# Tiles 4 to 15 transposed by one DMA each, with copies of x behind them, in a Fourier-mixing and MLP kernel

## The chip, the cores and the metric

The kernel runs on one core of a Trainium2 chip. The metric is the device time of one execution in microseconds (us). The median of three runs before the change is 1255.71 us. Engines: TensorE (PE: matmuls and transposes by matmul; PEld is its loading of weights), VectorE (DVE), ScalarE (ACT), GpSimd (POOL) and SyncE (SP). SP only issues DMAs here: loads, copies in DRAM and transposing DMAs. POOL issues the DMAs that accumulate into DRAM.

## The reference

With x of 2048 rows and 576 columns, xn its layer norm, Cr, Ci the real and imaginary DFT matrices of the sequence and Dr, Di those of the hidden dimension:

```
xn  = (x - mean) / sqrt(var + 1e-5)
a   = xn @ Dr.T ;  b = xn @ Di.T
y   = Cr @ a - Ci @ b
out = x + y + relu(xn @ w1) @ w2        # w1: 576 x 4608, w2: 4608 x 576
```

All in f32. Each factor of a product is held as two f16 tensors, `hi` and `lo` (the rounded value and the remainder), after a scale by a power of two, so each product is three f16 products.

## The kernel before, in words

The 2048 rows are 16 tiles of 128, and 4 groups of 4 tiles. The MLP's 4608 columns are 9 blocks of 512. For each block b and group g there is a first product (`mlp1`, line 324, or `pair_products`, line 479, from block 2 on) and a second one (`mlp2`, line 556): seven products (q = 0 to 6) after Strassen and Winograd, 12 matmuls each, with sums of h and of w2 made by VectorE. After the MLP come the DFTs (lines 1091 and 1210).

A framework builds the program: it tracks which tile is written and read, sets the semaphores, and orders each engine's instructions by a list schedule on its own cost estimates, in which the order of the text is the priority. `tc.issue_after(ins)`, and `behind(key)` on top of it, put the instructions of a block behind `ins` on the queue of the same engine. Queues run in order.

The change lies in what comes before and inside block 0, the first 100 us:

- Tile t of x is loaded (line 96); `stats` makes mean and variance on VectorE (205, 208), a square root on ScalarE (215), then the reciprocal and a Newton step on VectorE (216 to 227).
- `normalize` writes xn in f32 on VectorE (247) and its f16 `hi` on ScalarE (249) into a staging buffer `dbuf`. `remainder` makes `lo` (253, 256), on POOL for tiles 1 to 11 and on VectorE for tile 0 and tiles 12 to 15.
- The transposed tile has ten blocks of 128 by 128: four and a half of `hi`, the same of `lo`, and the last 128 columns of `hi` once more. `transposes` (tiles 0 to 7) does them by ten matmuls (272, 277) into PSUM and two ScalarE copies (279, 282). `transposes_dma` (tiles 8 to 15) issues two transposing DMAs from SP: nine blocks (265), and one block that needs `hi` alone (266).
- Group 0 and half of group 1 take the first product tile by tile (`tile_by`), the other half 512 wide (`mlp1`). `mlp1_out` makes relu, `hi`, `lo` and the sums (365 to 377).
- `prepare_w2` makes w2's scale and splits: sums of magnitudes on ScalarE (646), a maximum over partitions by matmul (`power_pe`, 152 to 175), small VectorE steps (657 to 671), then for both halves i the splits (182 on ScalarE, 183 on VectorE) and sums (678 to 681). They are the steps `w[0]` to `w[10]` and beyond in the text.
- `mlp2` of block 0 and group 0 runs q = 0 to 2, then the first two `mlp1` of group 2 (`early`), then q = 3 to 6. Its results go to `acc` (567, 570), and POOL adds them into DRAM buffers `spill` (573).
- `spill` is first filled with x: 16 copies from DRAM to DRAM, 288 KB each (line 760), issued on SP behind all loads of x.
- In the loop after that, the step n == 2 takes group 2 and prepares tiles 12 to 15. Block 1's w1 (107) and w2 (100) are loaded through SP there, w2 into buffers which the splits of block 1's w1 free. `first_c` (948) loads blocks of the sequence matrices for their scale.

Of the kernel before, what the change touches and what calls it, by code (L numbers as in the profile page):

```python
# [14 lines left out]
ALU = mybir.AluOpType  # L15
# [34 lines left out]
def kernel(  # L50
# [101 lines left out]
    def power_pe(s, p, m):  # L152

        n = m.shape[-1]
        ps = ps2.tile([P, 2, 512], F32, tag="ps2", name="pm")

        for c in range(n):
            nc.tensor.matmul(
                ps[:1, 0, c * P : (c + 1) * P], m[:, c : c + 1], ident.bitcast(BF16),
                start=True, stop=True,  # L160
            )
        top = small.tile([1, n], BF16, tag=f"top{n}", name="top")
        nc.vector.tensor_reduce(
            top, ps[:1, 0, : n * P].rearrange("p (n f) -> p n f", f=P), AX.X, ALU.max
        )
        nc.tensor.matmul(ps[:, 1, :n], ones, top, start=True, stop=True)
        half = small.tile([P, n], F32, tag=f"half{n}", name="half")
        nc.vector.tensor_scalar(half, ps[:, 1, :n], 2.0**-107, 2.0**6, ALU.max, ALU.mult)
        nc.vector.tensor_scalar(
            s.bitcast(I32), half.bitcast(I32), EXPONENT, EXPONENT,  # L170
            ALU.bitwise_and, ALU.bitwise_xor,
        )
        nc.vector.tensor_scalar(
            p.bitcast(I32), half.bitcast(I32), EXPONENT, None, ALU.bitwise_and
        )
# [4 lines left out]
    def split(hi, lo, src, s):  # L180

        nc.scalar.activation(hi, src, AF.Copy, scale=s)  # L182
        nc.vector.scalar_tensor_tensor(lo, src, s, hi, ALU.mult, ALU.subtract)  # L183


    xT = [xpool[g].tile([P, NKX + 1, G], F16, name=f"xT{g}") for g in range(NG)]
# [7 lines left out]

        return tc.issue_after(order[key]) if key in order else nullcontext()

    def stats(ts, after=None):

        n = len(ts)
        mv = small.tile([P, n, 2], F32, tag=f"mv{n}", name=f"mv{ts[0]}")  # L200
        sts = [small.tile([P, 2, 6], F32, tag="st", name=f"st{t}", bufs=4) for t in ts]
        for t, st in zip(ts, sts):
            for j in range(2):
                with behind(after):
                    nc.vector.bn_stats(st[:, j, :], acc[t][:, j * EH : (j + 1) * EH])
                yield
        for i, st in enumerate(sts):
            nc.vector.bn_aggr(mv[:, i], st.rearrange("p a b -> p (a b)"))
# [6 lines left out]
        order["root", ts[0]] = nc.scalar.activation(u, v, AF.Sqrt, bias=eps).ins  # L215
        nc.vector.reciprocal(r0, u)
        yield

        stt(u, v, EPS, r0, ALU.add, ALU.mult)
        yield  # L220
        nc.vector.tensor_tensor(u, u, r0, ALU.mult)
        yield
        nc.vector.tensor_scalar(u, u, -0.5 * SX, 1.5 * SX, ALU.mult, ALU.add)
        yield
        nc.vector.tensor_tensor(r, u, r0, ALU.mult)
        yield
        order["sh", ts[0]] = stt(sh, m, -1.0, r, ALU.mult, ALU.mult).ins
        for i, t in enumerate(ts):
            means[t], factors[t], shifts[t] = mv[:, i, 0:1], r[:, i : i + 1], sh[:, i : i + 1]
# [12 lines left out]
    def normalize(t, eng=nc.vector, after=None):  # L242
        stage = dbufs[t % 4]
        xn = xns[t] = stage[:, :D]

        xs = xss[t] = stage[:, D : 2 * D].bitcast(F16)
        eng.tensor_scalar(xn, acc[t], means[t], factors[t], ALU.subtract, ALU.mult)
        with behind(after):
            nc.scalar.activation(xs[:, :D], acc[t], AF.Identity, bias=shifts[t], scale=factors[t])

    def remainder(t, eng):
# [2 lines left out]
            xs[:, D : D + REM], xn[:, KM * P :], xs[:, KM * P : D], ALU.subtract  # L254
        )
        eng.tensor_tensor(
            xs[:, D + REM :], xn[:, : KM * P], xs[:, : KM * P], ALU.subtract
        )

    def transposes_dma(t):  # L260

        xs = xss[t]
        g, c = divmod(t, TG)
        dst = xT[g][:, :, c * P : (c + 1) * P]
        nc.sync.dma_start_transpose(dst[:, :NKX], xs)
        nc.sync.dma_start_transpose(dst[:, NKX], xs[:, D - P : D])

    def transposes(t):
        xs = xss[t]
        pt = ps2.tile([P, 2, 1024], F16, tag="ps2", name=f"pt{t}")  # L270
        for k in range(NKX):
            nc.tensor.transpose(
                pt[:, k // 8, (k % 8) * P : (k % 8 + 1) * P], xs[:, k * P : (k + 1) * P], ident
            )
        g, c = divmod(t, TG)

        nc.tensor.transpose(pt[:, 1, P : 2 * P], xs[:, D - P : D], ident)
        dst = xT[g][:, :, c * P : (c + 1) * P]
        nc.scalar.activation(
            dst[:, :8, :], pt[:, 0, :].rearrange("p (k t) -> p k t", t=P), AF.Copy  # L280
        )
        order["xT", t] = nc.scalar.activation(
            dst[:, 8:, :], pt[:, 1, : 2 * P].rearrange("p (k t) -> p k t", t=P), AF.Copy
        ).ins

# [71 lines left out]
    def mlp1_out(b, g, i, pa, pb, after=None):  # L357
# [8 lines left out]
        for q, src in ((slice(A11, A11 + 1), a11), (slice(A12, A22 + 1), pb)):  # L366
            hi, lo = (h[:, n, q].rearrange("p a b -> p (a b)") for n in range(2))
            with behind(after):
                nc.scalar.activation(hi, src, AF.Relu)
            stt(lo, src, 0.0, hi, ALU.max, ALU.subtract)  # L370
        stt(s3, a11, 0.0, r21, ALU.max, ALU.subtract)
        stt(s1, a22, 0.0, r21, ALU.max, ALU.add)
        stt(s2, a22, 0.0, s3, ALU.max, ALU.subtract)
        stt(s4, a12, 0.0, s2, ALU.max, ALU.subtract)
# [167 lines left out]
    def mlp2(b, g, n):  # L542
# [25 lines left out]
        else:  # L568
            o = sums[row, col]
            add = nc.vector.scalar_tensor_tensor(o, ps, us[b], o, ALU.mult, ALU.add)  # L570
            order["acc"] = order["vfree"] = add.ins
        if n not in (0, 2, 3):
            nc.gpsimd.dma_start(spill[g, row, col], o, accum_op=ALU.add)  # L573

# [2 lines left out]
    def max_w1(b, f):  # L577
# [6 lines left out]
        with behind("vfree" if b >= BB else ("sh", 1) if f > 1 else None):  # L584
# [65 lines left out]
    def power_w2(b):  # L650
# [2 lines left out]
            yield from power(*(t["w2", b] for t in (sc, pw, mx)))  # L653
        else:
            m = small.tile([P, NQ], BF16, tag="mb2", name=f"mb2_{b}")
            with behind(("sh", 8)):
                nc.vector.tensor_copy(m, mx["w2", b])
            power_pe(sc["w2", b], pw["w2", b], m)
        p1 = pw["w1", b]
# [26 lines left out]
    def split_w2(b, i, c):  # L686
# [5 lines left out]
        with behind(None if b else ("xT", 7)):  # L692
            split(w[:, 0, q], w[:, 1, q], src, sc["w2", b][:, i : i + 1])

    def long(f):

# [58 lines left out]
    load_w2(0, 1)  # L755
    for t in range(2 * TG, NT):
        load_x(t)
    for g, row, col in spill:
        src = x[(g * TG + row * 2) * P : (g * TG + row * 2 + 2) * P, col * EH : (col + 1) * EH]
        nc.sync.dma_start(spill[g, row, col], src.rearrange("(c p) e -> p c e", p=P))  # L760
    warm = const.tile([P, 1], F32, name="warm")
    nc.scalar.activation(warm, eps, AF.Sqrt)

# [6 lines left out]
            mlp1_group(0, g, i, slice(c * P, (c + 1) * P), ps[i], wk)  # L770

    no = lambda: None
    N, E, T, TD = normalize, remainder, transposes, transposes_dma

    def fill(n, src=idle):

# [31 lines left out]
    E(2, GP)  # L808
    tile_by(0, (2,), ps)
    tile_by(1, (2,), ps)  # L810
    T(2)
    split_w1(0, 3)
    N(3)
    E(3, GP)
    tile_by(0, (3,), ps)
    tile_by(1, (3,), ps)
    T(3)
    weave(stats([4, 5, 6, 7]))
    N(4)
    E(4, GP)  # L820
# [11 lines left out]
    T(5)  # L832
    tile_by(4, (0, 1), qs)
    mlp1_out(0, 0, 0, *ps[:2])
    T(6)
    tile_by(5, (0, 1), qs)
    T(7)
    weave(stats([8, 9, 10, 11], ("sh", 4)))
    N(8, after=("xT", 5))
    E(8, GP)  # L840
    mlp1_out(0, 0, 1, *ps[2:], after=("xT", 6))
    for t in (9, 10, 11):
        N(t, after=("xT", 7))
        E(t, GP)
    tile_by(6, (0, 1), qs)
    w[3]()
    tile_by(7, (0, 1), qs)
    w[4]()
    w[5]()
    mlp1_out(0, 1, 0, *qs)  # L850
    for f in w[6:]:
        f()
    TD(8)
    q2 = [mlp1(0, 1, 2)]
    TD(9)
    q2.append(mlp1(0, 1, 3))
    mlp1_out(0, 1, 1, *q2)
    TD(10)
    TD(11)
    for q in range(3):  # L860
        mlp2(0, 0, q)
    with tc.issue_after(order["pe"]):
        early = [mlp1(0, 2, 0), mlp1(0, 2, 1)]
    for q in range(3, 7):
        mlp2(0, 0, q)


# [77 lines left out]
    def first_c(m):  # L945
        n, q = divmod(m, 4)
        f = firsts[m] = mlp.tile([P, HK, P], F32, tag="first", name=f"f{n}_{q}", bufs=1)
        nc.sync.dma_start(f, blocks_c(n)[q])

    def sum_c(m):  # L950

# [11 lines left out]
    for n in range(2, len(steps)):  # L963
# [46 lines left out]
        for i in range(NF):  # L1010
# [267 lines left out]
```

## Time and profile before

| what | value |
|---|---|
| median of three runs | 1255.71 us (1254.37 to 1256.63) |
| the profiled execution's own time | 1256.51 us |
| its span | 1254.7 us |
| TensorE busy | 1234.3 us, 98% of the span |
| VectorE busy | 1008.9 us, 80% |
| ScalarE busy | 704.8 us, 56% |
| POOL busy | 155.6 us, 12% |
| mean granted TensorE clock | 0.999 |

In rows of the timeline, waits and groups, `L556` is line 556 of the kernel before. A wait reads "engine, tile, line <- what came last": total us, number of times, longest. A group's row gives output<-input, shape, count, then busy us and the mean in ns of one instruction, then the idle time ahead of it. Durations of neighbouring matmuls overlap, because they are pipelined. SPq is SP's queue of DMA issues; a time to landing runs from the issue to the completion.

### The profile page before, as it was taken

To read this page: it belongs to the slowest core of one execution; us is meant where nothing else is said; L and a number is where in the kernel's file an instruction comes from. 1 tells how busy PE (TensorE), PEld (TensorE's weight loads), DVE (VectorE), ACT (ScalarE), POOL (GpSimd) and SP (SyncE) were. 2 spreads that over 40 slices of the span, in tenths; PEclk is the share of its full clock that TensorE was granted. 3 is DMA by queue.
4 is the path that set the end of the run, shared out by engine and by line. 5 is a ranking of instruction groups with operands and counts; after the bars stand their busy time and mean duration, and the time that the engine had idled before them with its cause. 6 is when DMAs were issued, how large, how long until landed. Compare 5 with 4: busy or idle time off the path is not lost.

```text
span 1254.7 us, 25397 instructions
## 1 busy us (share of the span) xinstructions
PE 1234.3 (98%) x10309; PEld 983.5 (78%) x10309; DVE 1008.9 (80%) x1921; ACT 704.8 (56%) x1194; POOL 155.6 (12%) x199
## 2 busy tenths in 40 slices
PE   8799999999999999999999999999999999999998
PEld 7565657888888888888888888877777777777776
DVE  8999997878878778788787878566788878788885
ACT  5756566676666666766767666444453333333332
POOL 1321111212111111212121212100000000000000
PEclk9999999999999999999999999999999999999999
DMA  9576567666567665766576766630053434433420
GB/s 341 131 127 109 97 125 166 110 133 139 132 117 171 122 150 117 137 140 136 117 153 142 145 126 128 113 95 1 1 172 111 144 102 162 124 133 120 141 87 19
DMA packets 75909, 158.08 MB, mean 126 GB/s; under 512 B 17296, under 2 KB 36240, under 8 KB 75792
## 3 DMA queue, kind: packets, MB, share of 16 engines
q1 hardware_dynamic: 53008, 113.99, 28.3%
q0 software_dynamic: 22784, 42.48, 25.4%
q8 instruction: 80, 1.31, 0.4%
q14 instruction: 37, 0.30, 0.1%
HBM read 106.63 MB, written 51.90 MB: 126 GB/s over the span
## 4 chain that ended last, share of the span: by engine, by line
PE 74%; DVE 17%; DMA 4%; ACT 4%; issue 2%; POOL 0%; SPq 0%; DVEq 0%; ACTq 0%; POOLq 0%
PE p L1210 26%; PE p L556 19%; PE bank L479 19%; PE pd L1091 8%; DVE w2s L183 2%; DMA raw_w<-in_w_dram 1%; DMA acc<-in_x_dram 1%; DVE h L370 1%; PE p L324 1%; DVE h L501 1%; DVE h L377 1%; DMA f<-in_cre_dram 1%; ACT f L955 1%; DVE w1buf L183 1%; DVE dbuf L570 1%
## 5 line engine op out<-in xcount | busy, mean ns | idle before, releaser
L556 PE MATMUL p<-w2s,h 128*128 128x288 f16 x3024 | 409.8, 286 | 8.6 <-DVE w2s L183 3.3
L556 PEld LDWEIGHTS <-h 128*128 128x128 f16 x3024 | 295.5, 98 | 85.7 <-issue 9.8
L1210 PE MATMUL p<-R,cs 128*128 128x288 f16 x2688 | 329.4, 286 | 0.0
L1210 PEld LDWEIGHTS <-cs 128*128 128x128 f16 x2688 | 263.0, 98 | 66.3
L182 ACT ACTIVATE cs<-c,sc_c 128x1024 f16<-128x1024 f32 x112 | 125.1, 1144 | 196.8 <-DVE c L1153 72.6
L183 DVE SCALAR_TENSOR_TENSOR cs<-c,sc_c,cs 128x1024 f16<-128x1024 f32 x112 | 141.0, 1282 | 54.4 <-ACT cs L182 54.4
L479 PEld LDWEIGHTS <-w1buf 128*128 128x128 f16 x1600 | 156.5, 98 | 22.8 <-issue 1.7
L479 PEld LDWEIGHTS <-dbuf 128*128 128x128 f16 x1200 | 117.4, 98 | 17.5 <-issue 1.7
L479 PE MATMUL bank<-xT,w1buf 128*128 128x256 f16 x832 | 109.8, 273 | 0.0
L1091 PE MATMUL pd<-dbuf,xT 128*128 128x288 f16 x832 | 103.8, 286 | 0.0
L479 PE MATMUL bank<-acc,w1buf 128*128 128x256 f16 x768 | 102.1, 273 | 1.0 <-DVE acc L509 0.9
L1091 PEld LDWEIGHTS <-xT 128*128 128x128 f16 x832 | 80.8, 98 | 22.0 <-issue 1.9
L501 DVE TENSOR_TENSOR h<-s,h 128x1024 f16<-128x1024 f32 x56 | 68.5, 1223 | 33.9 <-ACT h L498 33.6
L573 POOL DMA_DIRECT2D spill<-dbuf x70 | 60.9, 875 | 233.1 <-DVE dbuf L570 201.9
L486 ACT ACTIVATE h<-acc 128x256 f16<-128x256 f32 x112 | 45.9, 411 | 77.5 <-DVE acc L509 74.8
L479 PE MATMUL bank<-xT,dbuf 128*128 128x256 f16 x624 | 82.4, 273 | 0.0
L498 ACT ACTIVATE h<-s 128x1024 f16<-128x1024 f32 x56 | 59.1, 1056 | 35.9 <-DVE s L493 35.1
L479 PE MATMUL bank<-acc,dbuf 128*128 128x256 f16 x576 | 76.6, 273 | 1.0 <-DVE acc L509 0.9
L1216 DVE SCALAR_TENSOR_TENSOR o<-p,us_c,o 128x288 f32<-128x288 f32 x112 | 57.5, 514 | 12.9 <-PE p L1210 12.3
L955 ACT ACTIVATE f<-f 128x1024 f32<-128x1024 f32 x64 | 66.9, 1046 | 0.6 <-DMA f<-in_cre_dram 0.6
L487 DVE SCALAR_TENSOR_TENSOR h<-acc,h 128x256 f16<-128x256 f32 x112 | 47.2, 422 | 21.0 <-ACT h L486 20.8
L573 POOL DMA_DIRECT2D spill<-sum x42 | 36.3, 865 | 184.9 <-DVE sum L570 159.8
(158 smaller groups left out, 1536.8 us busy)
## 6 DMA issues: line engine op xcount, KB each, us to landing
spill<-dbuf POOLq DMA_DIRECT2D x70, 288.0 KB, 5.2
f<-in_cre_dram SPq DMA_DIRECT2D x32, 512.0 KB, 5.8
f<-in_cim_dram SPq DMA_DIRECT2D x32, 512.0 KB, 5.2
c<-in_cre_dram SPq DMA_DIRECT2D x32, 512.0 KB, 4.1
c<-in_cim_dram SPq DMA_DIRECT2D x32, 512.0 KB, 5.0
spill<-sum POOLq DMA_DIRECT2D x42, 288.0 KB, 4.6
raw_w<-in_w_dram SPq DMA_DIRECT2D x17, 640.0 KB, 6.0
raw_w<-in_w_dram SPq DMA_DIRECT2D x18, 576.0 KB, 4.9
```

Source lines behind the costliest of these rows:

```text
L182: nc.scalar.activation(hi, src, AF.Copy, scale=s)
L183: nc.vector.scalar_tensor_tensor(lo, src, s, hi, ALU.mult, ALU.subtract)
L479: nc.tensor.matmul(ps, l, r, start=first and m == 0, stop=m == len(todo) - 1, skip_group_check=not first,)
L487: stt(lo, src, 0.0, hi, ALU.max, ALU.subtract)
L498: order["s"] = nc.scalar.activation(hi_s, st[:, 1:], AF.Copy).ins
L501: order["lo"] = nc.vector.tensor_tensor(lo_s, st[:, 1:], hi_s, ALU.subtract).ins
L556: order["pe"] = nc.tensor.matmul(ps[:, c], h[:, x, qa, c * P : (c + 1) * P], w[:, y, qb], start=first and i == 0 and j == 0, stop=i == NQ ...
L573: nc.gpsimd.dma_start(spill[g, row, col], o, accum_op=ALU.add)
L955: nc.scalar.activation(f, f, AF.Abs, scale=2.0**-10, accum_out=sums_c[:, n, q : q + 1])
L1091: nc.tensor.matmul(ps[j], xT[g][:, kx, c * P : (c + 1) * P], dsp[j][:, hl, k], start=(t % 2 == 0 and n == 0), stop=(t % 2 == 1 and n == le ...
L1210: nc.tensor.matmul(ps, w[:, a, k], r[:, c, rq], start=first and k == 0 and j == 0, stop=k == HK - 1 and j == 2, skip_group_check=not first,)
L1216: order["o"] = nc.vector.scalar_tensor_tensor(o, ps, us["c"][:, n : n + 1], o, ALU.mult, ALU.add).ins
```

## The change

- `transposes_dma` now serves tiles 4 to 15. The last 128 columns of `hi` are copied once more behind the `lo` part (POOL for tiles 4 to 11, ScalarE for tiles 12 to 15), so that one DMA with ten blocks does what two did. The DMAs are kept in their order of text by `behind("td")`.
- The f32 normalization of tiles 10, 11, 13 and 15 goes from VectorE to ScalarE.
- The copies of x into `spill` (`copy_x`) are issued behind the latest transposing DMA: group 0's after tile 11's, the twelve others after tile 15's. `first_c` goes behind it too.
- w2's maximum and scale (`w[3]`) come in front of the reciprocal of tiles 8 to 11, the first splits of both halves (`w[4]`, `w[6]`) behind the second `mlp1_out`, the sums and other splits behind those. `mlp1_out(0, 1, 1)` waits for the last split.
- `early` stands ahead of `mlp2` of group 0, which runs q = 0 to 6 in one go.
- The ScalarE copies of tile 2 (`copies`) go behind the square root of tiles 4 to 7.

The core of the diff:

```diff
+        again = xs[:, 2 * D :], xs[:, D - P : D]
+        if eng is nc.scalar:
+            eng.activation(*again, AF.Copy)
+        else:
+            eng.tensor_copy(*again)
+        with behind("td"):
+            order["td"] = nc.sync.dma_start_transpose(xT[g][:, :, c * P : (c + 1) * P], xs).ins
...
+    def copy_x(g):
+        for row, col in itertools.product(range(2), range(2)):
+            t = g * TG + row * 2
+            src = x[t * P : (t + 2) * P, col * EH : (col + 1) * EH]
+            with behind("td"):
+                nc.sync.dma_start(spill[g, row, col], src.rearrange("(c p) e -> p c e", p=P))
...
+    weave(stats([4, 5, 6, 7]))
+    copies(2, pt, ("root", 4))
     T(3)
...
-    for t in (5, 6, 7):
+    for t in (4, 5, 6, 7):
         N(t)
         E(t, GP)
-    T(4)
+        TD(t, GP)
     tile_by(3, (0, 1, 2, 3), ps)
+    rest = stats([8, 9, 10, 11], ("sh", 4), "top")
+    for _ in range(3 * TG):
+        next(rest)
+    w[3]()
+    weave(rest)
...
+    mlp1_out(0, 0, 0, *ps[:2], after="top")
+    with behind("pm"):
+        for t in (4, 5):
+            tile_by(t, (0, 1), qs)
+    for t in (8, 9):
+        N(t, after="s4")
         E(t, GP)
+        TD(t, GP)
+    mlp1_out(0, 0, 1, *ps[2:])
+    for t in (6, 7):
+        tile_by(t, (0, 1), qs)
+    for t in (10, 11):
+        N(t, nc.scalar, after="hi")
+        E(t, GP)
+        TD(t, GP)
     w[4]()
+    w[6]()
+    mlp1_out(0, 1, 0, *qs)
+    q2 = [mlp1(0, 1, 2), mlp1(0, 1, 3)]
     w[5]()
-    for f in w[6:]:
+    for f in w[7:]:
         f()
...
+    mlp1_out(0, 1, 1, *q2, after="w2")
+    copy_x(0)
+    early = [mlp1(0, 2, 0), mlp1(0, 2, 1)]
+    for q in range(7):
         mlp2(0, 0, q)
...
-                normalize(t)
+                normalize(t, nc.scalar if i % 2 else nc.vector)
                 remainder(t, nc.vector)
-                transposes_dma(t)
+                transposes_dma(t, nc.scalar)
...
         if n == 2:
+            for k in range(1, NG):
+                copy_x(k)
             for q in range(7):
                 mlp2(pb, pg, q)
```

More of the change, by code (lines that the diff above doesn't have):

```diff
@@ L162, in power_pe @@
         top = small.tile([1, n], BF16, tag=f"top{n}", name="top")
-        nc.vector.tensor_reduce(
+        order["top"] = nc.vector.tensor_reduce(
             top, ps[:1, 0, : n * P].rearrange("p (n f) -> p n f", f=P), AX.X, ALU.max
-        )
-        nc.tensor.matmul(ps[:, 1, :n], ones, top, start=True, stop=True)
+        ).ins
+        order["pm"] = nc.tensor.matmul(ps[:, 1, :n], ones, top, start=True, stop=True).ins
         half = small.tile([P, n], F32, tag=f"half{n}", name="half")
@@ L215, in stats @@
         order["root", ts[0]] = nc.scalar.activation(u, v, AF.Sqrt, bias=eps).ins
-        nc.vector.reciprocal(r0, u)
+        with behind(late):
+            nc.vector.reciprocal(r0, u)
         yield
@@ L274, in transposes, with copies @@
             )
+        nc.tensor.transpose(pt[:, 1, P : 2 * P], xs[:, D - P : D], ident)
+        return pt
+    def copies(t, pt, after=None):
         g, c = divmod(t, TG)
-        nc.tensor.transpose(pt[:, 1, P : 2 * P], xs[:, D - P : D], ident)
         dst = xT[g][:, :, c * P : (c + 1) * P]
[L279 to L284, printed above, removed]
+        with behind(after):
+            nc.scalar.activation(
+                dst[:, :8, :], pt[:, 0, :].rearrange("p (k t) -> p k t", t=P), AF.Copy
+            )
+            nc.scalar.activation(
+                dst[:, 8:, :], pt[:, 1, : 2 * P].rearrange("p (k t) -> p k t", t=P), AF.Copy
+            )
     A11, A12, A22, S1, S2, S3, S4 = range(7)
@@ L368, in mlp1_out @@
             with behind(after):
[L369 to L374, printed above, removed]
+                order["hi"] = nc.scalar.activation(hi, src, AF.Relu).ins
+                stt(lo, src, 0.0, hi, ALU.max, ALU.subtract)
+        with behind(after):
+            stt(s3, a11, 0.0, r21, ALU.max, ALU.subtract)
+            stt(s1, a22, 0.0, r21, ALU.max, ALU.add)
+            stt(s2, a22, 0.0, s3, ALU.max, ALU.subtract)
+            order["s4"] = stt(s4, a12, 0.0, s2, ALU.max, ALU.subtract).ins
         hi, lo = (h[:, n, S1 : S4 + 1] for n in range(2))
@@ L571, in mlp2 @@
             order["acc"] = order["vfree"] = add.ins
+            order.setdefault("add", add.ins)
         if n not in (0, 2, 3):
@@ L583, in max_w1 @@
             mx["f", b] = cell("mf", 2)
-        with behind("vfree" if b >= BB else ("sh", 1) if f > 1 else None):
+        with behind("vfree" if b >= BB else "add" if b else ("sh", 1) if f > 1 else None):
             magnitude(mx["f", b][:, r : r + 1], raws["w1", b, i][:, r * KT : (r + 1) * KT])
@@ L772, with T @@
     no = lambda: None
-    N, E, T, TD = normalize, remainder, transposes, transposes_dma
+    N, E, TD = normalize, remainder, transposes_dma
+    def T(t):
+        copies(t, transposes(t))
     def fill(n, src=idle):
@@ L810 @@
     tile_by(1, (2,), ps)
-    T(2)
+    pt = transposes(2)
     split_w1(0, 3)
```

63 lines of the change are left out of this document (15 added, 48 removed).

## The prediction

> **What bounds the kernel now.** I read the page's table of engines first, then the table by stages, then the waits of TensorE (PE) and VectorE (DVE) in the first 200 us, because the diff touches nothing after that.
>
> The page's row for TensorE:
> ```profile
> PE 1234.3 (98%) x10309; PEld 983.5 (78%) x10309; DVE 1008.9 (80%) x1921; ACT 704.8 (56%) x1194; POOL 155.6 (12%) x199
> ```
> TensorE is busy for 98% of the span, so only some 20 us of idle time are left anywhere. The table by stages tells where. Each row gives a stretch in us, its length, then busy time (and count) of PE, PEld, DVE, ACT, POOL, the granted clock, the DMA share (1.0 is all 16 engines) and GB/s:
> ```profile
> 34.00:50.00 16.00, 15.09 (x176) 10.85 (x174) 15.17 (x39) 13.01 (x24) 7.17 (x10) 1.00 0.55 125
> 50.00:62.00 12.00, 5.79 (x36) 3.51 (x35) 12.00 (x23) 6.21 (x9) 0.00 (x0) 0.96 0.36 90
> 62.00:75.40 13.40, 13.40 (x79) 7.86 (x78) 12.14 (x34) 6.46 (x11) 3.62 (x5) 0.91 0.33 71
> 75.40:92.00 16.60, 16.52 (x114) 10.95 (x112) 16.39 (x35) 8.61 (x14) 4.09 (x4) 1.00 1.13 173
> 92.00:112.00 20.00, 20.00 (x127) 11.85 (x125) 19.08 (x42) 13.94 (x23) 3.64 (x4) 1.00 0.57 98
> 112.00:200.00 88.00, 86.42 (x543) 51.29 (x541) 83.46 (x166) 52.53 (x88) 17.08 (x19) 1.00 0.62 120
> ```
> From 50 to 62 us TensorE works for 5.79 of 12 us while VectorE works for all 12. That is the hole in the profile. And VectorE stays nearly full until 200 us: what TensorE gains early it can keep only as far as VectorE comes along. Its room is 0.2 us up to 92, 0.9 up to 112 and 4.5 up to 200.
>
> TensorE's waits from 33 to 75 us (total, times, longest):
> ```profile
> PE p L556 <- DVE w2s L183: 3.3, 4, 1.1
> PE p L556 <- ACT w2s L182: 2.4, 2, 1.9
> PE pm L158 <- DVE mb L657: 0.6, 1, 0.6
> PE p L556 <- DVE s L374: 0.5, 1, 0.5
> PE p L324 <- ACT xT L279: 0.3, 1, 0.3
> ```
> The second MLP product of block 0 waits for the splits of w2 (lines 182 and 183). The five sum to 7.1 us.
>
> VectorE's waits from 22 to 200 us, the four largest:
> ```profile
> DVE h L370 <- ACT h L369: 3.8, 2, 1.9
> DVE r L216 <- ACT u L215: 2.1, 1, 2.1
> DVE acc L570 <- ACT dbuf L249: 1.2, 1, 1.2
> DVE w2s L183 <- ACT w2s L182: 1.1, 1, 1.1
> ```
> TensorE in order of time after the hole (start, us from first to last, count at the end):
> ```profile
> 62.10 7.42 PE L324 MATMUL p<-xT,w1buf 128*128 128x512 f16 x28
> 69.36 6.04 PE L556 MATMUL p<-w2s,h 128*128 128x288 f16 x48
> 75.24 6.21 PE L324 MATMUL p<-xT,w1buf 128*128 128x512 f16 x28
> 81.28 10.74 PE L556 MATMUL p<-w2s,h 128*128 128x288 f16 x84
> 91.86 0.38 PE L324 MATMUL p<-xT,w1buf 128*128 128x512 f16 x1
> ```
> The same 28 matmuls take 7.42 us right after the hole and 6.21 us later; the clock column stands at 0.96 and 0.91 around it. The hole costs 1.2 us more than its own length.
>
> **The change, part by part.** The sum is made for TensorE first, then checked against VectorE, then charged for the moved copies.
>
> *Transposes of tiles 4 to 7 leave TensorE.* One tile's set of ten, and what follows it:
> ```profile
> 33.93 0.67 PE L272 MATMUL pt<-ident,dbuf 128*128 128x128 f16 x9
> 34.43 0.22 PE L277 MATMUL pt<-ident,dbuf 128*128 128x128 f16 x1
> 34.49 1.73 PE L324 MATMUL p<-xT,w1buf 128*128 128x128 f16 x28
> ```
> From 33.93 to 34.49 is 0.56 us, so four tiles give 2.2 us. ScalarE (ACT) loses the two copies out of PSUM for each; from 33 to 41 us:
> ```profile
> L279 ACT ACTIVATE xT<-pt 128x1024 f16<-128x1024 f16 x4 | 4.1, 1018 | 0.0
> L282 ACT ACTIVATE xT<-pt 128x256 f16<-128x256 f16 x4 | 1.5, 384 | 0.0
> ```
> That is 5.6 us less. It takes on the f32 normalization of tiles 10, 11, 13 and 15 (at most 1.02 us each, by the wider L279) and four small copies in the later groups (at most 0.38 each), 5.6 us at most. With 13.01 of 16 us and 6.21 of 12 us used, ScalarE covers that; I cost it at nothing.
>
> *Tiles 4 to 15 come by one DMA transpose each.* Sixteen issues become twelve. Before, line 265 moved nine of the ten blocks; its summary has
> ```profile
> DMA to landing us min/median/max: 3.2/3.8/6.5
> ```
> A tile on TensorE's way took 0.56 us and two copies (1.4 us). Now tile 4 must pass normalization, the remainders on POOL, the new POOL copy and one landing of about 4 us. TensorE's work on tile 3 covers part of that. Left bare it would cost 3.8 us, fully covered nothing; I take 2, because only the first of the four is bare: the others follow at POOL's pace, below 28 matmuls (1.73 us) each. Tiles 8 to 11 land under the twenty-eight 512-wide matmuls before `early`; without that cover, up to 3.8 us.
>
> *The POOL copy.* Remainders from 33 to 48 us:
> ```profile
> L256 POOL TENSOR_TENSOR dbuf<-dbuf 128x512 f16<-128x512 f32 x6 | 7.2, 1194 | 0.0
> L253 POOL TENSOR_TENSOR dbuf<-dbuf 128x64 f16<-128x64 f32 x5 | 1.7, 350 | 5.7 <-PE pt L277 4.6 <-ACT dbuf L249 1.1
> ```
> 128 columns lie between 0.35 and 1.19 us; on the line between them 0.47, so eight copies are 3.8 us of POOL, which idles around them. What they may do to VectorE is a rival below.
>
> *w2's scale and splits sooner, `early` in front of the product.* The scale's chain follows the statistics instead of the normalization, the first splits no longer wait for tile 7, and 28 matmuls (6.2 us) that stood between q = 2 and q = 3 now stand ahead of q = 0. Together they cover the 7.1 us of waits, and with the hole goes the 1.2 us of slow clock. The new waits, the PSUM matmul `pm` ahead of tile 4 and the reciprocal behind `top`, stall only queues that then hold work for the same tiles. The bounds of this term are 0 (the splits still end last) and 8.3; I take 8.3, since the splits need only be about 6 us nearer. Seven products in a row may wait for line 570's add, at most one such instruction; I take 0.
>
> TensorE: 2.2 + 8.3 - 2 = 8.5 us.
>
> *VectorE.* Tile 2's copies now go behind the square root, so the 2.1 us of line 216 go; at 32 to 34 us statistics and scale now fill one of the two waits of line 370 (1.9). Four normalizations leave VectorE:
> ```profile
> 40.00 0.57 DVE L247 TENSOR_SCALAR dbuf<-acc,mv,r 128x576 f32<-128x576 f32 x1
> 40.48 1.13 DVE L657 CAST mb<-c_mw 128x2 bf16<-128x2 f32 x1
> ...
> 44.81 0.70 DVE L169 TENSOR_SCALAR c_tw<-half 128x2 int32<-128x2 int32 x1
> 45.42 0.16 DVE L173 TENSOR_SCALAR c_pw<-half 128x2 int32<-128x2 int32 x1
> ```
> Four times 0.57 is 2.3. So VectorE reaches tile 15 sooner by 2.1 + 1.9 + 2.3 = 6.3 us (2.3 if the waits return). TensorE's next group at 91.86 us needs all of tiles 12 to 15, which VectorE prepares, so VectorE's 6.3 counts and not 8.5.
>
> *The copies of x.* Sixteen DRAM copies now run early; the queue's row, and the DMA share from 18 to 38 us in 40 slices:
> ```profile
> 18.07 12.77 SPq L760 DMA_DIRECT2D spill<-in_x_dram  x16
> ```
> ```profile
> DMA  9999999999999999999999999999999998830000
> ```
> They fill all DMA engines for about 18 us, 1.1 us each. There they hide; they would stand in front of tile 4's transpose, and one of the things bought is that they don't. Four go behind tile 11, under the MLP products. Twelve go behind tile 15: 9.6 us of SP's issue (12.77/16 each) and 13.5 us of full DMA, into a stretch whose share is already 1.13. What stands behind them on SP is w2 of block 1 (L100):
> ```profile
> 80.68 5.46 SPq L265 DMA_TRANSPOSE xT<-dbuf  x3
> 88.44 7.67 SPq L100 DMA_DIRECT2D raw_w<-in_w_dram  x2
> ```
> and ScalarE already waits for it; the page's list of issues has the size and the median time to landing of such a load below that:
> ```profile
> 101.21 1.16 ACT L646 ACTIVATE j<-raw_w 128x1152 f32<-128x1152 f32 x1 [1.23 <-DMA raw_w<-in_w_dram]
> ```
> ```profile
> raw_w<-in_w_dram SPq DMA_DIRECT2D x18, 576.0 KB, 4.9
> ```
> POOL's accumulating DMAs of group 1 wait for the copies as well, but what reuses that buffer comes later, with block 1's sums of x. Price of the copies: 0 if the loads pass, 13.5 if all are in front and unshared. With tile 15 at 79 us the copies end near 93; the second load, wanted at 95 and about 5 us long, lands near 98. I take 3, of which VectorE's room up to 200 us (5.4) gives back 2.
>
> Sum: 6.3 - 1 = 5.3 us. The profiled execution took 1256.51 us (span 1254.7 and 1.8 around it), so it would be 1251.2; the median, 1255.71, lies 0.8 lower, so 1250.4.
>
> **The rivals.**
> *All of TensorE's gain is kept* (0.14). The tile waits hide, the w2 load passes, VectorE uses its room: 2.2 + 8.3 = 10.5 us, 1245. For it: 5.4 us of VectorE's room after 92 us; against it: VectorE at 16.39 of 16.60 before tile 15.
>
> *POOL's copies hold VectorE, or tile 4 stays bare* (0.18). The cast of two columns took 1.13 us and line 169 took 0.70 while POOL ran remainders; the same shape took 0.16 at line 173. Eight copies of 0.47 us, each stopping one VectorE instruction for its length, take 3.8 of the 6.3: a gain of 1.5, 1254. [...]
>
> *The copies of x take the place of the hole* (0.17), which ends slower. If the twelve copies share the engines evenly with POOL's accumulating DMAs, 13.5 us become 27, the second w2 load lands near 108 and ScalarE stands; VectorE's scale and splits of block 1 and TensorE's second product follow in order. It decides from a landing at 101, as now: there all of the gain is spent. At 106 to 108 it is 1260. For it: the share of 1.13; against it: after 92 us the share falls to 0.57. [...]
>
> *The scheduler leaves the order as it was* (0.05): w2's splits still end last, only the transposes go, 2.2 us: 1253.5.
>
> **How the numbers follow.** The forecast has 0.46 and a range of its own of 1247 to 1253. Measurement here tells 0.2% (2.5 us) from no change. Faster: nearly all of 0.46, 0.14, and a third of the 0.23 of the third and fifth case, 0.66. Same: the rest of those, 0.15. Slower: 0.17 and a tail, 0.19. The range for eight in ten goes from 1244 (just past the full gain) to 1259 (most of the slower case).
>
> **What would show it.** After the change: no line 272 rows after tile 3; TensorE's busy time near full from 50 to 62 us and the clock at 1.00 behind it; one wait of 1 to 3 us for an SP transpose ahead of tile 4; `early` ahead of line 556; VectorE past tile 15 about 6 us sooner; ScalarE's wait on w2 of block 1 at 95 to 100 us, 1 to 4 us. Wrong if that wait is above 7 us, if TensorE stands for tiles 8 to 11, if short VectorE rows around 30 to 45 us grow to about 1 us, or if after tile 15 TensorE runs ahead and VectorE's idle time closes fully.

## The result and the profile after

The kernel with the change takes 1265.2 us (median; 1264.76 to 1265.63) against 1256.17 us for the kernel before on the same chip: a ratio of 1.0071 (95% interval 1.0054 to 1.0089). It is 9 us slower, where 5 us of gain were forecast. The profiled execution took 1264.97 us with a span of 1263.2.

TensorE's total work barely moved (1234.3 us before):

```profile
PE 1233.8 (98%) x10269; PEld 982.1 (78%) x10269; DVE 1007.9 (80%) x1917; ACT 703.8 (56%) x1194; POOL 160.8 (13%) x207
```

So the loss is idle time in the sum. The table by stages, with the columns of the prediction, shows where:

```profile
50.00:62.00 12.00, 10.19 (x43) 4.70 (x44) 8.86 (x18) 4.15 (x7) 0.00 (x0) 0.72 0.72 212
62.00:75.40 13.40, 13.40 (x95) 9.08 (x93) 11.11 (x31) 5.57 (x10) 4.65 (x4) 1.00 0.55 75
75.40:92.00 16.60, 12.49 (x71) 7.92 (x70) 14.02 (x31) 11.41 (x18) 2.00 (x3) 0.79 0.87 185
92.00:112.00 20.00, 17.41 (x113) 10.49 (x111) 13.48 (x24) 8.52 (x16) 4.35 (x4) 1.00 1.02 267
```

The hole of 50 to 62 us is smaller (10.19 us of work, 5.79 before, though now at a clock of 0.72), but from 75.4 to 112 us TensorE, which had been full, works for 29.90 of 36.60 us, and the DMA share from 92 to 112 us is 1.02 (0.57 before). TensorE in order of time; in brackets stand the idle time ahead of a row and what ended it:

```profile
34.46 12.54 PE L336 MATMUL p<-xT,w1buf 128*128 128x128 f16 x140 [2.31 <-DMA xT<-dbuf]
51.81 8.63 PE L336 MATMUL p<-xT,w1buf 128*128 128x512 f16 x28 [4.82 <-DMA xT<-dbuf]
...
76.61 3.10 PE L569 MATMUL p<-w2s,h 128*128 128x288 f16 x24
82.99 2.05 PE L569 MATMUL p<-w2s,h 128*128 128x288 f16 x12 [3.28 <-ACT acc L580]
85.86 5.54 PE L569 MATMUL p<-w2s,h 128*128 128x288 f16 x24 [0.83 <-ACT acc L580]
...
113.10 3.10 PE L569 MATMUL p<-w2s,h 128*128 128x288 f16 x24 [3.69 <-ACT acc L580]
...
120.90 2.97 PE L336 MATMUL p<-xT,dbuf 128*128 128x512 f16 x13
```

(Line 336 after is line 324 before, 569 is 556, 580 is 567.) Three things are to be seen. A stand (TensorE idle) for tile 4 and one for tiles 8 to 11 have replaced the waits for w2's splits. At 76.61 us the second product of group 1 begins, 4.7 us ahead of before (81.28). Then two losses undo that and more: the waits for line 580, ScalarE's emptying of PSUM, at 80 us with the slow rows behind them, and the wait ahead of 113.10 us. Behind the last one is ScalarE, which stands for a load:

```profile
110.68 1.16 ACT L660 ACTIVATE j<-raw_w 128x1152 f32<-128x1152 f32 x1 [6.71 <-DMA raw_w<-in_w_dram]
...
112.32 1.36 ACT L580 ACTIVATE acc<-p,c_ub 128x576 f32<-128x576 f32 x2
```

That load is the second half of block 1's w2. SP's queue shows it behind the twelve copies (line 779):

```profile
85.27 3.31 SPq L779 DMA_DIRECT2D spill<-in_x_dram  x5
88.86 0.38 SPq L100 DMA_DIRECT2D raw_w<-in_w_dram  x1
89.28 6.62 SPq L779 DMA_DIRECT2D spill<-in_x_dram  x7
98.81 0.33 SPq L100 DMA_DIRECT2D raw_w<-in_w_dram  x1
```

It was issued at 98.81 us and landed 11.8 us later; in the kernel before it was issued at 95.8 and landed in about 5. So some 3 us of its lateness are the issue and some 7 the landing. The issue itself was not held by the copies, whose last one SP had issued by 95.90: SP waited 2.7 us until VectorE's splits of block 1's w1 (line 183, from 97.11 us, 1.68 long) had freed the buffer. In the list of issues from 60 to 120 us (size, median us to landing) both it and the copies are long:

```profile
spill<-in_x_dram SPq DMA_DIRECT2D x12, 288.0 KB, 8.5
...
raw_w<-in_w_dram SPq DMA_DIRECT2D x2, 576.0 KB, 9.5
```

### The profile page after: what moved, and what is told of

It reads as the page before. It is cut to its first block, busy times and chain, and to the rows that moved or that the text cites. A ratio compares the mean times of both kernels' runs of the same rounds, so it can differ in the third digit from the quotient of the medians.

```text
span 1263.2 us, 25306 instructions
## 1 busy us (share of the span) xinstructions
PE 1233.8 (98%) x10269; PEld 982.1 (78%) x10269; DVE 1007.9 (80%) x1917; ACT 703.8 (56%) x1194; POOL 160.8 (13%) x207
## 4 chain that ended last, share of the span: by engine, by line
PE 80%; DVE 13%; ACT 3%; DMA 2%; issue 2%; POOL 1%; SPq 0%; DVEq 0%; ACTq 0%; POOLq 0%
PE p L1233 26%; PE p L569 22%; PE bank L492 21%; PE pd L1114 8%; PE p L336 2%; DVE w2s L183 1%; DMA raw_w<-in_w_dram 1%; DVE w1buf L183 1%; DVE dbuf L453 1%; DVE h L382 1%; DVE h L514 1%; ACT w2s L182 1%; ACT dbuf L253 0%; DVE acc L438 0%; DVE sum L583 0%
## 5 line engine op out<-in xcount | busy, mean ns | idle before, releaser
L336 PE MATMUL p<-xT,w1buf 128*128 128x128 f16 (+1 forms) x472 | 53.1, 271 | 8.8 <-DMA xT<-dbuf 7.1
```

The costliest lines, as they stand in the source:

```text
L336: nc.tensor.matmul(ps[:, cols], w1s[b, i // 2][:, hl, i % 2 * KT + k], xT[g][:, kx, cols], start=(start and n == 0), stop=(stop and n == l ...
```

## The experiments

Three suspects follow from this profile: the place of the copies, ScalarE's queue around tiles 12 to 15 (it now has normalizations ahead of line 580), and POOL's longer work on tiles 8 to 11. "Before" in a ratio is the kernel before on the same chip; edits are against the kernel with the change unless said otherwise.

**Tiles 13 and 15 normalized on VectorE again.** The extra copy of tiles 12 to 15 goes to VectorE too.

```diff
-                normalize(t, nc.scalar if i % 2 else nc.vector)
+                normalize(t)
-                transposes_dma(t, nc.scalar)
+                transposes_dma(t, nc.vector)
```

> One part undone: tiles 13 and 15 are normalized on VectorE again, and the copy of the last columns of tiles 12 to 15 runs on VectorE instead of ScalarE. Theory (the ScalarE queue): in the changed kernel TensorE stands 3.3 and 0.8 us near 80 to 86 us because the emptying of PSUM (line 580) is queued on ScalarE behind these six moved instructions, and the stand brings 2 to 3 us of half clock; without them 4 to 7 us come back: 1258 to 1261, against 1265.2. Rival (VectorE is the bound there): VectorE gets 1.6 us more to do, nothing comes back, 1265 to 1268.

Measured: 1266.77 us, ratio 1.0079 (1.0062 to 1.0095), no better than the change itself. TensorE's first wait for line 580 near 80 us fell from 3.28 to 1.17 us, but a wait of 2.9 us for VectorE came instead, so that TensorE's row of 106.45 us in the change comes at 106.77. Behind that, ScalarE's wait for w2 grew from 6.7 to 9.4 us and TensorE's for line 580 from 3.69 to 5.54. Whether VectorE's extra work or the late load kept the gain away, this run alone doesn't tell; the fifth run answers it.

**All sixteen copies right behind the loads of x.**

```diff
+    for k in range(NG):
+        copy_x(k)
     warm = const.tile([P, 1], F32, name="warm")
...
-    copy_x(0)
...
-            for k in range(1, NG):
-                copy_x(k)
```

> One part undone: all sixteen copies of x are issued right behind the loads of x, as before the change; all else as changed. Theory (the copies stand in front of block 1's w2): the wait of 6.7 us of ScalarE for w2 near 110 us goes, 4 to 6 us come back, but the transposes of tile 4 land behind the copies and TensorE stands 3 to 5 us more near 34 us: 1261 to 1265. Rival (the copies cost nothing, block 1 is late through VectorE): 1265 or more.

Measured: 1261.79 us, 1.0040 (1.0027 to 1.0052). ScalarE's wait for w2 fell from 6.7 to 1.3 us, but now tile 4's transpose stands behind the copies: TensorE waits 6.5 us for it, and 5.2 us later on, at 92.41. The order of time puts the second wait down to nothing that it names ("issue"); the view of line 274 puts it down to the transposing DMAs of tiles 12 to 15, which landed in 3.3 to 10.1 us here (median 7.6, in the change 3.6).

**Half the copies in front, half behind tile 11.**

```diff
+    for k in range(2):
+        copy_x(k)
     warm = const.tile([P, 1], F32, name="warm")
...
-    copy_x(0)
+    for k in range(2, NG):
+        copy_x(k)
...
-            for k in range(1, NG):
-                copy_x(k)
```

> The copies of groups 0 and 1 are issued right behind the loads of x, where the changed kernel leaves the DMA engines idle from 20 to 30 us, those of groups 2 and 3 behind tile 11's transpose, none behind tile 15's. Theory (copies in front of w2): ScalarE's wait for w2 falls from 6.7 to below 2 us and 4 to 6 us come back, 1259 to 1261, if block 1's w1, now behind eight copies, still lands before 64 us. Rival (VectorE bound): 1264 to 1266.

Measured: 1256.23 us, 1.0003 (0.9994 to 1.0012). The same work with the copies elsewhere is 9.0 us faster than the change and level with before. SP's queue, the issues from 60 to 120 us, and TensorE's rows that answer to those above:

```profile
17.74 5.47 SPq L779 DMA_DIRECT2D spill<-in_x_dram  x8
...
50.32 5.27 SPq L779 DMA_DIRECT2D spill<-in_x_dram  x8
...
87.33 7.59 SPq L100 DMA_DIRECT2D raw_w<-in_w_dram  x2
```
```profile
raw_w<-in_w_dram SPq DMA_DIRECT2D x2, 576.0 KB, 4.7
```
```profile
52.43 7.89 PE L336 MATMUL p<-xT,w1buf 128*128 128x512 f16 x28 [3.29 <-DMA xT<-dbuf]
...
81.63 1.63 PE L569 MATMUL p<-w2s,h 128*128 128x288 f16 x12 [2.03 <-ACT acc L580]
84.09 3.10 PE L569 MATMUL p<-w2s,h 128*128 128x288 f16 x24 [0.83 <-ACT acc L580]
...
112.25 2.97 PE L336 MATMUL p<-xT,dbuf 128*128 128x512 f16 x13
```

The load lands in 4.7 us instead of 9.5, and the wait at 113 us is gone: that is about 4.4 of the 8.65 us between 112.25 and 120.90. The other 4.2 come at 80 us: there the wait for line 580 is 2.03 instead of 3.28 us, and the 36 matmuls behind it run at full speed (a clock of 1.00 from 76 to 92 us; 1.63 + 3.10 us against 2.05 + 5.54). Why tiles 12 to 15 are also sooner here, when only copies moved, no run separates: other instructions changed places in the schedule as well.

**The kernel before, with only its copies moved to the change's places.**

```diff
-        nc.sync.dma_start_transpose(dst[:, :NKX], xs)
+        order['td'] = nc.sync.dma_start_transpose(dst[:, :NKX], xs).ins
...
-    for g, row, col in spill:
+    def copy_x(g):
+      for row, col in itertools.product(range(2), range(2)):
...
+        with tc.issue_after(order['td']):
+          nc.sync.dma_start(spill[g, row, col], src.rearrange("(c p) e -> p c e", p=P))
...
     TD(11)
+    copy_x(0)
...
         if n == 2:
+            for k in range(1, NG):
+                copy_x(k)
```

> One part done alone, on the kernel before: the copies of x of group 0 are issued behind tile 11's transposing DMAs and the twelve others behind tile 15's, nothing else is changed. Theory (the late copies are the whole loss): the second load of w2 of block 1 lands late, ScalarE waits 6 to 9 us for it where it waited 1.2, and the time rises by 6 to 9 us, 1262 to 1265. Rival (the loss needs the rest of the change): the kernel before has more room behind tile 15, 1255 to 1258.

Measured: 1269.03 us, 1.0095 (1.0073 to 1.0117), 12.4 us slower than before. This is the other side of the same test, and its waits from 90 to 130 us name the same chain, ScalarE's wait first and TensorE's after it (646 and 567 are the lines of before):

```profile
ACT j L646 <- DMA raw_w<-in_w_dram: 11.5, 1, 11.5
```
```profile
PE p L556 <- ACT acc L567: 8.5, 1, 8.5
```

Of the 12.0 us by which TensorE is late at the mark of the table below, 10.7 arise behind 105 us, in this chain; 1.3 are there at 82.55 us already, ahead of the twelve copies. So the late copies cost 9.0 us in the change and 12.4 us where they are the only edit, and with the copies by halves the rest of the change wins nothing. The other runs ask where its 5 to 8 us went.

**Half the copies in front, and tiles 13 and 15 on VectorE again** (the edits of the first and third run together).

> The copies as in the run before this one, and tiles 13 and 15 and the extra copies on VectorE as in the first. If the two causes are separate and both real, the gains add: 9 to 12 us less than the changed kernel, 1253 to 1256, as fast as the kernel before the change. If VectorE bounds the stretch from 75 to 200 us, 1264 to 1267.

Measured: 1260.79 us, 1.0034 (1.0023 to 1.0046), 4.6 us slower than with ScalarE's normalization. TensorE's waits for line 580 fell to 0.8 us, but it waits 3.80 us for a transposed tile at 88.98. ScalarE's wait for w2 is only 1.6 us here, so the late load hides no gain: this work costs more on VectorE than on ScalarE.

**The extra copy of tiles 8 to 11 on ScalarE, copies by halves.** On top of the third run:

```diff
         E(t, GP)
-        TD(t, GP)
+        TD(t, nc.scalar)
```

in both loops, over tiles 8, 9 and 10, 11.

> Half of the copies early and half behind tile 11, as in the earlier run of that kind, and the extra copy of the last columns of tiles 8 to 11 made on ScalarE instead of POOL. Theory (POOL's chain makes tiles 8 to 11 late): POOL has 1.2 to 2.6 us less between 37 and 48 us, tile 11 lands 2 us sooner, TensorE's wait of 3.3 us for it falls to about 1 and the half clock behind it shortens: 1252 to 1254 against 1256.2. Rival (VectorE is the bound from 50 to 200 us): no gain, 1255 to 1258.

Measured: 1256.80 us, 1.0000 (0.9991 to 1.0010). TensorE in order of time:

```profile
49.84 6.20 PE L336 MATMUL p<-xT,w1buf 128*128 128x512 f16 x28 [0.78 <-ACT h L381]
...
73.23 3.10 PE L569 MATMUL p<-w2s,h 128*128 128x288 f16 x24
82.94 9.66 PE L569 MATMUL p<-w2s,h 128*128 128x288 f16 x60 [6.60 <-ACT acc L580]
```

The stand for tiles 8 to 11 is gone: POOL's copy was its cause. TensorE is then 8.0 us ahead of before at the second product of group 1 (73.23 against 81.28), which is nearly the 8.5 us forecast for it, and loses all of it in one wait of 6.60 us and at a lower clock behind it (0.79 on the mean of 76 to 92 us; 60 matmuls in 9.66 us, where 72 had taken 8.99).

**`early` behind q = 1, copies by halves.** On top of the third run:

```diff
-    early = [mlp1(0, 2, 0), mlp1(0, 2, 1)]
-    for q in range(7):
+    for q in range(2):
+        mlp2(0, 0, q)
+    with tc.issue_after(order["pe"]):
+        early = [mlp1(0, 2, 0), mlp1(0, 2, 1)]
+    for q in range(2, 7):
         mlp2(0, 0, q)
```

> Copies half early, half behind tile 11, and the first two products of group 2 not ahead of the second product of group 0 but behind its q = 1. Theory (TensorE's stand for tiles 8 to 11 is worth its length): 24 matmuls, 3.1 us, fill the stand of 3.3 us, the clock stays full (1.7 us), 1251 to 1253 against 1256.2. Rival (VectorE is the bound): 1255 to 1257, or more because the sums of group 2 come later on VectorE.

Measured: 1256.39 us, 1.0000 (0.9990 to 1.0009). The stand for tiles 8 to 11 is gone here too, but VectorE waits 3.8 us for the load of block 1's w1, TensorE 3.85 for VectorE, and again 2.03 and 0.83 for line 580. (This profile is of an execution of 1259.36 us, 3 us above the median, so these waits need not stand in the others.)

**Both edits.** 

> Both edits that take away TensorE's stand for tiles 8 to 11, together. Theory V (tiles 12 to 15 are ready when VectorE is, and VectorE is no sooner): TensorE's lead grows to 8 to 10 us at 73 us and is given back by 92 us; 1256, ratio 0.999 to 1.001. Rival T (TensorE's lead counts, each of the two edits alone only moved one wait to another): 1252 to 1254, ratio 0.997 to 0.998.

Measured: 1252.93 us, 0.9968 (0.9957 to 0.9980): the theory that VectorE takes back whatever TensorE gains falls, and this version is 0.3% faster than the kernel before. TensorE keeps its lead:

```profile
73.58 3.10 PE L569 MATMUL p<-w2s,h 128*128 128x288 f16 x24
78.82 1.63 PE L569 MATMUL p<-w2s,h 128*128 128x288 f16 x12 [2.14 <-ACT acc L580]
81.28 3.10 PE L569 MATMUL p<-w2s,h 128*128 128x288 f16 x24 [0.83 <-ACT acc L580]
...
109.80 2.97 PE L336 MATMUL p<-xT,dbuf 128*128 128x512 f16 x13
```

It starts that product no sooner than with the extra copy on ScalarE alone (73.23), but line 580 comes 4.1 us sooner. ScalarE in order of time from 78 to 83 us, first with the extra copy on ScalarE alone, then with both edits:

```profile
79.02 0.81 ACT L182 ACTIVATE dbuf<-raw_w,c_sw 128x640 f16<-128x640 f32 x1
...
81.20 1.06 ACT L389 ACTIVATE h<-s 128x1024 f16<-128x1024 f32 x1 [0.45 <-DVE s L387]
82.16 0.72 ACT L580 ACTIVATE acc<-p,c_ub 128x576 f32<-128x576 f32 x1
```
```profile
78.04 0.73 ACT L580 ACTIVATE acc<-p,c_ub 128x576 f32<-128x576 f32 x1
...
80.49 0.74 ACT L580 ACTIVATE acc<-p,c_ub 128x576 f32<-128x576 f32 x1 [0.39 <-PE p L569]
81.62 1.55 ACT L182 ACTIVATE dbuf<-raw_w,c_sw 128x640 f16<-128x640 f32 x2 [0.40 <-DVE c_sw L125]
```

In the slower one, two splits of block 1's w1 (line 182), the extra copy between them and the sums' `hi` (389) stand ahead of line 580, in the faster one behind it.

**The remainders of tiles 12 to 15 on POOL,** all four, and then only tiles 13 and 15, on top of the run with the extra copy on ScalarE:

```diff
-                remainder(t, nc.vector)
+                remainder(t, nc.gpsimd)
```

> The copies in front by halves and the extra copy of tiles 8 to 11 on ScalarE, and the remainders of tiles 12 to 15 on POOL instead of VectorE: 3.6 us of VectorE's rows between 66 and 92 us leave it (2.7 of line 260, 0.9 of line 257). Theory V (VectorE's work sets the end of tiles 12 to 15): TensorE's stand of 6.6 us there shrinks by about 3 us, 1253 to 1254, ratio 0.997 to 0.998. Rival Q (ScalarE's queue holds the emptying of PSUM, whatever VectorE does): 1256 to 1257. Rival C (POOL's remainders of 1.2 us beside VectorE hold it, and the tiles land later): VectorE's rows of two inputs grow to 1 us and more, 1258 to 1260, ratio 1.001 to 1.003.

> As the run with all four remainders on POOL, but only tiles 13 and 15 go there: 1.8 us leave VectorE. Theory V: half the gain, 1254 to 1255.5, ratio 0.998 to 0.999. Rival Q: 1256 to 1257. Rival C: half the loss, 1257 to 1258.

Measured: 1261.19 us, 1.0038 (1.0026 to 1.0050), and 1259.49 us, 1.0025 (1.0016 to 1.0035). Less work for VectorE made it slower, by more than the third theory said (1258 to 1260 and 1257 to 1258). The longer rows that this theory named are there: POOL takes 1.26 us where VectorE took 0.68, and line 450, a row of two inputs on VectorE, took 1.53 us beside it in both runs, 0.69 in the run that they were made from. With all four on POOL:

```profile
87.79 1.53 DVE L450 TENSOR_TENSOR dbuf<-dbuf,xT 128x512 f32<-128x512 f32 x1
```

But something larger came first, which no theory had. POOL's first remainder in order of time, with all four on POOL and with two:

```profile
84.15 0.30 POOL L257 TENSOR_TENSOR dbuf<-dbuf 128x64 f16<-128x64 f32 x1 [7.17 <-ACT acc L580]
```
```profile
83.88 0.30 POOL L257 TENSOR_TENSOR dbuf<-dbuf 128x64 f16<-128x64 f32 x1 [7.11 <-issue]
```

In the run that they were made from, VectorE began its four at 74.97 to 81.21 us (line 260). On POOL they stood behind its reduction for block 1's w1 (line 121), which ended at 76.98 and 76.77 us, and a gap of 7 us followed it; what fills the gap the profile doesn't say. The transposing DMAs followed from 85.58 and 85.31 us on (in the second run all but the first), against 75.71 to 83.29. So these two runs don't tell what less work on VectorE is worth.

**q = 0 of group 1's second product ahead of tile 15's normalization,** once on the run with the extra copy on ScalarE, once on the fastest version:

```diff
                 t = (g + 1) * TG + i
+                if i == 3:
+                    mlp2(pb, pg, 0)
...
-            for q in range(7):
+            for q in range(1, 7):
                 mlp2(pb, pg, q)
```

> The copies by halves in front, the extra copy of tiles 8 to 11 on ScalarE, and the first of the seven products of group 1 (q = 0 of its second product) placed ahead of tile 15's normalization in the text, so that ScalarE empties its PSUM (line 580) ahead of tile 15's normalization, two splits of block 1's w1 and a copy of sums, which were ahead of it. Theory Q (the order of ScalarE's queue holds PSUM and gave back the 8 us lead): TensorE's stand of 6.6 us at 76 us shrinks to 2 us or less, and the time goes to 1252 to 1254, ratio 0.997 to 0.998. Rival V (VectorE's work on tiles 12 to 15 is the end in any order): the stand moves to a wait for tile 15 or for VectorE, 1256 to 1257, ratio 0.999 to 1.001.

> The same edit on the fastest version (copies by halves in front, extra copy of tiles 8 to 11 on ScalarE, early behind q = 1): it still stood 2.14 and 0.83 us at 76 to 82 us for line 580. Theory Q: those 3 us go as well, 1250 to 1251, ratio 0.995 to 0.996. Rival V: VectorE, 15.93 of 16 us busy there, is the end now; the same 1252.9, ratio 0.996 to 0.998.

Measured: 1256.44 us, 1.0007 (0.9998 to 1.0017), and 1251.75 us, 0.9967 (0.9955 to 0.9978). In the first, the wait at 77 us shrank from 6.60 to 1.94 us as the queue theory had it, but the second emptying then stood at 82.99 behind the same splits and sums, TensorE waited 3.33 us for it, and nothing was won. In the second, the wait of 2.14 us became 0.51; the ratio is that of the version it was made from, so no further gain is shown. By these waits the lead is lost in ScalarE's queue. That its order is the cause is not shown, since moving one instruction of it didn't win the lead back in the first run. What else makes the version with both edits faster stays open: its statistics of tiles 12 to 15 also start 1.5 us sooner than in the version with one edit.

**All runs in one table.** The mark is the start of the first thirteen wide matmuls that read `dbuf` (114.05 us before), in each profiled execution.

| kernel | median us | ratio | mark against before, us | span against before, us |
|---|---|---|---|---|
| the change | 1265.2 | 1.0071 | +6.9 | +8.5 |
| tiles 13, 15 on VectorE | 1266.77 | 1.0079 | +10.5 | +10.9 |
| all copies in front | 1261.79 | 1.0040 | +6.4 | +6.7 |
| copies by halves | 1256.23 | 1.0003 | -1.8 | -1.2 |
| the same, 13, 15 on VectorE | 1260.79 | 1.0034 | +3.4 | +4.5 |
| before, copies late | 1269.03 | 1.0095 | +12.0 | +11.8 |
| halves, extra copy on ScalarE | 1256.80 | 1.0000 | +0.5 | +0.3 |
| halves, `early` behind q = 1 | 1256.39 | 1.0000 | +3.0 | +2.9 |
| halves, both | 1252.93 | 0.9968 | -4.3 | -3.4 |
| remainders on POOL | 1261.19 | 1.0038 | +2.8 | +3.9 |
| two remainders on POOL | 1259.49 | 1.0025 | +2.1 | +1.7 |
| extra copy on ScalarE, q = 0 first | 1256.44 | 1.0007 | +0.7 | +0.9 |
| both, q = 0 first | 1251.75 | 0.9967 | -5.7 | -6.2 |

The last two columns agree within 1.7 us in every row: what TensorE has won or lost at the mark is nearly the result. (The profiled execution of the eighth row took 1259.36 us, 3 us above its median.)

## Why the prediction was wrong, step by step

*What bounds the kernel.* The hole of 50 to 62 us was the right place to gain, and TensorE's sum of 8.5 us can be had there: the six versions with the extra copy of tiles 8 to 11 on ScalarE are 7.5 to 8.6 us ahead at the second product of group 1 (73.76 to 72.67 against 81.28). The change itself reached 4.7.

*Tile 4* was charged 2 us and took 2.31. The DMA transposes land as estimated; the tile's own view for 30 to 70 us has, for the eight of tiles 4 to 11:

```profile
DMA to landing us min/median/max: 3.4/3.5/4.1
```

*Tiles 8 to 11* "land under the twenty-eight 512-wide matmuls before `early`": this failed. TensorE stood 4.82 us for them, more than the 3.8 named as the price without cover, and the 28 matmuls behind took 8.63 instead of 6.21 us. POOL set the pace; its groups from 33 to 50 us:

```profile
L257 POOL TENSOR_TENSOR dbuf<-dbuf 128x64 f16<-128x64 f32 x5 | 3.3, 663 | 0.0
L272 POOL COPY dbuf<-dbuf 128x128 f16<-128x128 f16 x6 | 3.2, 529 | 2.1 <-ACT dbuf L253 2.1
```

The copy by itself takes 0.30 us, less than the 0.47 worked out, but one of them took 1.29 us (at 43.52) beside VectorE's line 390 (1.28 us, at 43.37), and the remainder of 64 columns went from 350 to 663 ns on the mean. The rival on POOL named rows that grow where both engines work, and put the price in the wrong place: tiles 8 to 11 wait for POOL's rows. VectorE's grew too, but only here and there: line 675 took 0.85 us at 34.53 (median 0.16), line 390 took 1.77 us at 38.90 (median 1.22). These two are 0.69 and 0.55 us over their medians. That every copy stops a VectorE instruction for its length was the author's estimate; whether either engine holds the other, no run separates.

*"VectorE reaches tile 15 sooner by 6.3 us"* failed. Its remainder of tile 15 starts at 83.13 us (84.17 before), 1.0 us sooner, and the statistics of tiles 12 to 15 start 2.5 us later. VectorE in order of time, first before, then after:

```profile
65.21 2.97 DVE L205 BATCH_NORM_STATS2 st<-acc 128x6 f32<-128x288 f32 x8
```
```profile
58.53 0.82 DVE L183 SCALAR_TENSOR_TENSOR w2s<-raw_w,c_sw,w2s 128x576 f16<-128x576 f32 x1 [2.42 <-ACT w2s L182]
...
63.50 0.82 DVE L583 SCALAR_TENSOR_TENSOR acc<-p,c_ub,acc 128x576 f32<-128x576 f32 x1 [2.22 <-PE p L569]
...
67.75 0.81 DVE L205 BATCH_NORM_STATS2 st<-acc 128x6 f32<-128x288 f32 x2
```

The four normalizations left VectorE as counted and the early waits shrank (of the 2.1 us for the square root 0.4 is left), but the two waits in these rows took their place: ScalarE's relu of `early` stood ahead of the last split of w2 and itself waited for TensorE's stand, and then TensorE's product was late for VectorE. With the stand gone, in the version with both edits, the statistics start at 64.12 us. The diff has one more order here that the list of the change leaves out: VectorE's maxima of block 1's w1 (line 115), 1.54 us ahead of the statistics, are put behind the first add of line 583, the row that waited 2.22 us. No run takes that back.

*ScalarE "covers that; I cost it at nothing"* failed. The prediction looked at ScalarE's room between 34 and 62 us; the normalizations of tiles 13 and 15 and the four small copies fall into 76 to 82 us, where it is full, ahead of the emptying of PSUM. ScalarE in order of time:

```profile
76.59 0.85 ACT L253 ACTIVATE dbuf<-acc,sh,r 128x576 f16<-128x576 f32 x1
...
81.46 0.85 ACT L253 ACTIVATE dbuf<-acc,sh,r 128x576 f16<-128x576 f32 x1
82.22 0.72 ACT L580 ACTIVATE acc<-p,c_ub 128x576 f32<-128x576 f32 x1
```

From 76.59 to 82.22 ScalarE has no gap. Yet giving the work back to VectorE costs 4.6 us.

*The copies of x, "I take 3, of which VectorE's room gives back 2":* this is the term that decided the sign. It measured 9.0 us (the change against copies by halves; 4.4 of them in the wait behind the load, 4.2 at 80 us by a way that stays open) and 12.4 us alone. The rival "The copies of x take the place of the hole" had the chain, and decided from a landing at 101 us; the load landed at about 110.6 (106 to 108 was worked out), and the time was 5 us beyond its 1260. That the copies and POOL's accumulating DMAs share the engines evenly was its assumption, which no run shows. Three details of the step were off. The second load was wanted at 104 us (110.68 less the wait of 6.71), not at 95, and was issued only at 98.81, when its buffer came free, 3 us later than before; it still met the copies. The full DMA stretch lasts to about 109 us, not 93; the list of issues has ten accumulating DMAs of POOL, block 1's w2 and a load of 512 KB beside the copies. And VectorE's room gave nothing back, as the table of marks shows. Of the step's two bounds, 0 if the loads pass and 13.5, the runs lie nearer the second: the load took 9.5 us behind the copies and 4.7 without them.

*The signs.* The stand for tiles 8 to 11 came. ScalarE's wait for w2, 6.71 us, was above the 1 to 4 forecast but just under the limit of 7 that was to show an error; a loss of 9 us went with it, so the limit was too wide.

## What to carry to other kernels

A DMA with no reader close by is not free to move (the late copies cost 9.0 us here): ask which load stands behind it on the same queue at the new place, how full the engines are there, and who waits for that load. When an engine "has room" on average, look at its queue at the very place where the moved work lands, and at what stands behind it there: from 76.59 to 82.22 us ScalarE had no gap here, and TensorE stood 3.28 us for line 580, which came at 82.22. PSUM that is emptied by the same engine is TensorE's work in disguise. And a lead won early counts only from the last place where the engines meet: one mark behind it, read in each profile, told the result of every version here to within 1.7 us.

## What the runs showed of the hardware beyond that

A stand can cost more than its length, but its length alone doesn't tell whether it will. The table by stages of the changed kernel, in short stretches, has the clock at 0.50 in the stretch in which the stand of 4.82 us ends, at 0.67 in the one in which that of 3.28 us ends, and at 1.00 in the one in which that of 3.69 us ends:

```profile
50.00:56.00 6.00, 4.19 (x10) 1.46 (x11) 6.00 (x12) 3.06 (x4) 0.00 (x0) 0.50 0.85 234
...
82.00:88.00 6.00, 4.18 (x22) 2.63 (x22) 6.00 (x16) 4.48 (x7) 0.35 (x1) 0.67 1.03 199
...
112.00:118.00 6.00, 4.90 (x34) 3.24 (x34) 5.55 (x15) 4.33 (x8) 0.36 (x1) 1.00 0.01 3
```

Behind the 3.28 us the next 36 matmuls took 7.59 us, 2.9 more than the 4.73 us of the same ones with the copies by halves; behind the 3.69 us, 24 of them took 3.10, full speed. Stands of 2.03 and 2.14 us at the place of the 3.28 were followed by full speed in two versions (24 in 3.10 us), but in the version with `early` behind q = 1 a stand of 2.03 us was not: the 12 behind it took 2.44 us (1.63 at full speed) and the next 24 took 5.15.

```profile
83.52 2.44 PE L569 MATMUL p<-w2s,h 128*128 128x288 f16 x12 [2.03 <-ACT acc L580]
```

What decides whether the clock falls behind a stand, no run separates.

Twelve copies in DRAM of 288 KB doubled the time of a 576 KB load behind them (median of two: 9.5 against 4.7 us, 10.7 in the kernel before with its copies late). A full DMA share alone doesn't do that: with the copies by halves it was 90% or more in every slice of 1.5 us from 87 to 97.5 us too, and there the load took 4.7 us. Whether the copies delay it by their place ahead of it or by what they ask of the DMA engines, no run separates.
